# A new order for a fused gated-linear-attention and bilinear-FFN kernel: alphas sent a block early, decays by pairs of heads, all orders searched anew

## The chip, the cores and the metric

One core of a Trainium2 chip. The time is in device microseconds (us) of one execution. TensorE (PE) multiplies matrices and has a separate row in the profile for its weight loads (PEld); VectorE is DVE, ScalarE is ACT, GpSimd is POOL, and SyncE (SP) issues DMAs. Every engine takes its instructions in the order written, and waits at an instruction whose semaphore has not come.

## The reference

Attention with a gated state, then a bilinear feed-forward block (FFN) on all its outputs:

```python
B, H, S, D = 4, 8, 768, 48
state = zeros(B, H, D, D)
for t in range(S):
    state = alpha[:, :, t, :, None] * state + einsum('bhd,bhe->bhde', k[:, :, t], v[:, :, t])
    y[:, :, t] = einsum('bhd,bhde->bhe', q[:, :, t], state)

x = y.transpose(0, 2, 1, 3).reshape(3072, 384)
out = (x @ w_a) * (x @ w_b) @ w_out     # w_a, w_b: 384 x 1536, w_out: 1536 x 384
```

Inputs and output are float32.

## The kernel before

The sequence is cut into 3 stretches of 256 positions, and the 4 batches into 2 pairs: six chunks of 512 rows. Chunk c holds stretch c // 2 and batches 2 * (c % 2) and the next. One position in two is an "even" row (r = 0), the other "odd" (r = 1), and 128 such pairs lie on the partitions; 64 of them make a group g.

For a chunk, the attention part runs in these steps, each a name in a program text:

- `ld` loads alpha, k, q or v. `ln` takes the logarithm of alpha (ACT, L586), `A` or (`l2`, `H`, `L`, `A2`, `le`) add it up along the sequence on PE with a triangle of ones. `E` takes exponentials (ACT, L646): `beta` is the decay from the start of the group, `invb` its inverse.
- `mk` and `mq` multiply keys by `invb` and queries by `beta` (DVE, L650) into `QKp`. They are turned so that the head dimension lies on the partitions: `C` on PE (L690) with the copy `Ce` (L696, L698) for chunks 0 and 1, and `T`, a DMA transpose issued by SP (L701), for chunks 2 to 5.
- `D` makes scores on PE (L758), `M` masks them (DVE, L763), `SB` and `SA` add the carried state (L774), `Y` the inner products (L774), and `X` copies the result to `xT` (L809).
- `K` and `k` make the new state (L729, L743 to L747). The decay of a whole group, `bl`, comes from the last row of `beta`: `dk` and `de` do that on PE and a copy for chunks 0 and 1, `dec` by a DMA through DRAM (L655, L658) for the others.

The FFN part has, for each of 12 column blocks f of 128, `a` and `b` (PE, L825, three matmuls each), `as` (ACT copies a, L831), `pr` (DVE multiplies by b, L838 or L841), then `o` (PE, L848) for 4 row blocks m, `ot` (a copy, L856 or L858) and `st` (the store, L865). With `*` a step of `a` takes all 512 columns, with 0 or 1 half of them (256): the halves let the first FFN work start when half of `xT` is there.

`x v S` and the like end with the engine's letter: V is DVE, S is ACT, P POOL, Y SP. A number at the end is the PSUM bank. Weights come by `W` and `Wo`, cast during the DMA, which POOL issues. `warm` is a matmul on zeros that has no other purpose than to run. `gatet` is a copy of one element on POOL that waits for a turned key, so that loads after it are not sent while the transposes run.

The order of all of this on every engine is the order of a text, `PROGRAM`, that the kernel interprets: `c: op; op; ...` for chunk c. Nothing else schedules it; waits come from the data and the buffers. Here are the steps around the gates of chunk 2 before:

```
2: K * 6; gatet 0
...
2: gatet 1
...
3: ld a * P
...
3: ld k * P
```

All loads of a chunk go to two buffers for each of a, k, q and v. `beta` and `invb` have one buffer each. The PSUM has eight banks that the text names by hand.

Of the kernel before, what the change touches and what calls it, by code (L numbers as in the profile page):

```python
# [18 lines left out]
0: ld a 0 Y; ld a 1 Y; cm 0; cm 1; ld k 0 Y; ld v 0 Y; cS 1 V; cQ 1 V; cM 0 V; cV 0 V; ln 0; ld q 0 P; cM 1 V; A 0 1 4; ld k 1 P; cQ 0 V; ln 1  # L19
0: cS 0 V; ld q 1 P; A 0 0 2; E 0 i1; ld v 1 P; E 0 b1; A 1 1 5  # L20
1: ld a 0 P
0: E 0 i0; E 0 b0; mk 0 V
1: ld a 1 P
0: A 1 0 4; E 1 i1; v 0 V; W b 0 256; E 1 b1; mq 0 V; dk 0 6; W a 0 256; E 1 i0; K 0 0; E 1 b0; dk 1 7; W a 256 1024; C 0 0 2; de 0 S; mk 1 V
0: W b 256 1024; de 1 S; Ce 0 0 S; C 0 1 7
1: ld k 0 P
0: k 0 0 V; warm 2 3; k 0 1 V; Ce 0 1 S; D 0 0 2
1: ld v 0 P
0: warm 2 4; mq 1 V; SB 0 0
1: ld q 0 P  # L30
0: D 0 1 6; v 1 S; M 0 0; C 1 0 5; W a 1024 1536; warm 2 4; Ce 1 0 S; M 0 1; W b 1024 1536; K 1 2; C 1 1 4; Wo 0 6; k 1 0 V; D 1 0 6; Ce 1 1 S
1: ld k 1 P
0: Y 0; SA 0; k 1 1 V; M 1 0
1: ld q 1 P
0: SB 1 4; D 1 1 2; X 0 S; Wo 6 12
1: ln 0
0: M 1 1
1: ld v 1 P; ln 1
0: a 0 0 6
# [3 lines left out]
0: as 0 0  # L43
1: H 0 V; L 0 V
0: b 0 0 6; X 1 S
2: ld k * P
1: l2 1 V; A2 0 1; H 1 S; le 0
2: ld q * P
1: E 0 b1
0: pr 0 0; a 6 * 7  # L50
1: E 0 i1; L 1 V
0: a 7 * 5
2: ld v * P
1: E 0 b0
0: cV 1 V; a 0 1 3; a 1 0 0; as 0 1; b 0 1 4; as 1 0; b 1 0 2; pr 0 1; as 6 *; a 3 0 1; pr 1 0
1: A2 1 6
0: as 3 0; b 6 * 3
1: le 1; E 0 i0
0: b 3 0 0
1: E 1 b1  # L60
0: pr 6 *; b 7 * 1; as 7 *
1: mk 0 V
0: a 4 * 2
1: E 1 i1
0: a 3 1 3; pr 3 0; b 3 1 7; as 3 1
1: dk 0 4
0: pr 7 *; as 4 *; b 4 * 6; pr 3 1
1: v 0 S
0: a 5 * 0
1: mq 0 V  # L70
0: b 5 * 7; as 5 *
1: de 0 V; C 0 1 3
0: pr 4 *; a 2 0 1
1: Ce 0 1 S; C 0 0 2
0: pr 5 *; b 2 0 4; a 8 * 5
1: Ce 0 0 V
0: as 2 0
1: E 1 b0; K 0 6
0: pr 2 0; as 8 *
1: D 0 0 2  # L80
0: a 11 * 0
1: k 0 0 V; M 0 0
0: b 11 * 4; as 11 *; a 10 * 5
1: k 0 1 V; E 1 i0; SB 0 2; D 0 1 0
0: as 10 *; b 8 * 6
1: M 0 1
0: b 10 * 7
1: dk 1 5
0: pr 8 *
1: Y 0; SA 0; de 1 S  # L90
0: pr 11 *; a 9 * 0; pr 10 *
1: X 0 S
0: b 9 * 6; as 9 *
1: b 11 0 3; a 1 0 2
0: pr 9 *
1: a 2 0 0; as 1 0; b 1 0 4; mk 1 V; as 2 0
0: a 2 1 1
1: b 2 0 6
0: as 2 1
1: a 4 0 2; pr 1 0  # L100
0: b 2 1 5
1: pr 2 0; as 4 0; a 8 0 7
0: pr 2 1
1: b 4 0 1; as 8 0; a 6 0 6; pr 4 0; b 6 0 2; as 6 0; mq 1 V; b 10 0 7; b 8 0 0; a 9 0 6; pr 8 0
0: a 1 1 5
1: as 9 0
0: b 1 1 1
1: pr 6 0
0: as 1 1
1: a 11 0 4; b 9 0 0  # L110
0: pr 1 1
1: as 11 0; C 1 0 6; pr 9 0; v 1 S; a 10 0 2; Ce 1 0 V; a 5 0 5; C 1 1 4; as 10 0; pr 11 0; as 5 0; K 1 0; pr 10 0; D 1 0 2
0: o 1 0 5
1: k 1 0 V; M 1 0
2: ln *
0: o 2 0 7; o 2 1 -
1: Ce 1 1 S
2: l2 * V
1: a 0 0 3; k 1 1 V
0: o 1 1 -  # L120
2: H * S
1: as 0 0
2: L * V
1: SB 1 0
0: ot 2 S
1: b 5 0 3
0: ot 1 S
1: pr 5 0
2: A2 0 7
1: D 1 1 4  # L130
2: le 0; E 0 i1
1: b 0 0 2
2: E 0 b1; A2 1 6
1: M 1 1
0: o 0 0 3
2: E 0 b0; E 1 b1; le 1
1: Y 1; SA 1
2: E 1 i1; dec; mq 0 V; E 0 i0
0: o 0 1 -
1: X 1 S  # L140
2: mk 0 V; E 1 i0
1: b 3 0 6; pr 0 0; b 11 1 0
2: E 1 b0; T 0
1: a 3 0 1
2: mk 1 V
1: a 8 1 4; as 3 0; a 11 1 2; as 8 1; a 9 1 5; pr 3 0; as 11 1; a 4 1 1
2: mq 1 V
1: b 8 1 4
0: ot 0 S
1: a 7 0 6; as 9 1; b 9 1 7; pr 11 1  # L150
2: T 1; v 1 S
1: b 7 0 3; pr 8 1; a 7 1 5
0: st 0 YY
2: v 0 V
1: b 2 1 0; as 4 1; b 7 1 2; as 7 0; pr 9 1; b 4 1 4; a 3 1 1; as 7 1
0: st 2 YY
1: pr 4 1
2: K * 6; gatet 0
1: pr 7 0; as 3 1; pr 7 1
2: D 0 0 4  # L160
0: st 1 YY
1: a 2 1 3
2: k * 0 V
0: o 3 0 2
1: as 2 1
2: M 0 0
1: a 0 1 3
0: o 3 1 -
2: gatet 1
1: as 0 1  # L170
3: ld a * P
2: k * 1 V
1: b 0 1 3
0: ot 3 S
1: b 3 1 5
3: ld k * P
1: a 1 1 4; pr 3 1; a 6 1 2; pr 2 1; a 5 1 7; as 1 1
3: ld q * P
1: a 10 1 1; pr 0 1; as 5 1; b 1 1 5; as 10 1; b 10 1 4; pr 1 1; b 5 1 7
3: ld v * P  # L180
1: pr 10 1; b 6 1 6; as 6 1
2: D 1 0 0
1: pr 5 1
2: SB 0 4
1: pr 6 1
2: D 0 1 2
1: o 2 0 7
2: M 0 1
1: o 2 1 -
2: M 1 0  # L190
3: ln *
2: Y 0; SA 0
1: ot 2 S
3: l2 * V
2: SB 1 0; D 1 1 2; X 0 S
1: o 1 0 6; st 2 YY
3: H * V
1: o 0 0 5
0: st 3 YY
3: L * V  # L200
1: o 1 1 -
2: M 1 1
3: A2 0 4
1: ot 1 S
3: A2 1 7; le 0
2: Y 1; SA 1
3: E 0 b1
1: st 1 YY
3: le 1; E 0 b0
1: o 0 1 -  # L210
3: mq 0 V
2: X 1 S
3: E 1 b1
2: b 11 * 0
1: ot 0 V
3: E 1 b0; dec
2: a 11 * 3
3: E 1 i1; mq 1 V
2: a 0 * 1
3: E 1 i0  # L220
2: as 11 *; b 6 * 7
3: mk 1 V; E 0 i0
2: a 6 * 5; pr 11 *; as 0 *
3: T 1
2: b 0 * 2; as 6 *
3: v 1 V
2: a 7 * 3
3: E 0 i1
2: pr 0 *; a 4 * 6
3: v 0 S; mk 0 V  # L230
2: a 5 * 5; as 7 *; b 7 * 2; pr 6 *
3: T 0
2: as 4 *; a 1 * 4; pr 7 *; as 5 *; b 5 * 7; as 1 *; b 4 * 3; pr 5 *; b 1 * 2; pr 4 *
3: D 1 0 6
2: pr 1 *
3: K * 4; M 1 0
2: a 2 * 1; b 2 * 3
3: gatet 0
2: as 2 *
3: gatet 1; k * 0 V  # L240
4: ld a * P
2: a 10 * 0; a 3 * 6; as 10 *
4: ld k * P
3: k * 1 V
1: o 3 0 2
2: as 3 *
4: ld q * P
2: pr 2 *
3: SB 1 0; D 1 1 6; D 0 0 4
1: o 3 1 -  # L250
3: M 1 1
4: ld v * P
2: a 8 * 3
3: M 0 0
1: ot 3 S
3: Y 1; SA 1
2: as 8 *
3: SB 0 2; D 0 1 4; X 1 S
2: b 8 * 7
3: M 0 1  # L260
4: ln *
2: b 9 * 6; a 9 * 0; pr 8 *
3: Y 0; SA 0
4: l2 * V
2: b 10 * 1
4: H * V
3: X 0 S
2: b 3 * 4
4: L * V
3: b 11 * 2  # L270
2: pr 10 *
3: a 8 * 7
2: pr 3 *
3: b 8 * 3; as 8 *
4: A2 0 5
2: as 9 *
4: A2 1 1; le 0
3: b 0 * 7
4: E 1 b1
3: pr 8 *  # L280
2: o 2 0 4
4: E 0 b0
2: pr 9 *
4: E 0 i1
3: a 1 * 3
4: E 0 b1; le 1; E 1 i1
3: a 0 * 0
4: dec; mq 0 V; E 0 i0
3: a 6 * 6
4: E 1 b0; mk 0 V  # L290
2: o 2 1 -
3: as 6 *
4: v 1 V; E 1 i0
3: b 4 * 1
4: T 0
2: ot 2 S
4: mk 1 V
2: o 1 0 6
3: as 1 *
4: mq 1 V  # L300
3: as 0 *
2: o 1 1 -
4: v 0 S; T 1
3: b 6 * 5
1: st 0 YY
3: a 11 * 3; pr 6 *; b 1 * 4
2: ot 1 V
3: as 11 *
2: st 2 YY
3: a 4 * 0; pr 1 *  # L310
4: gatet 0
3: a 5 * 3; pr 0 *; as 4 *
1: st 3 YY
3: b 3 * 6; pr 11 *; as 5 *; a 10 * 4; pr 4 *; b 5 * 0; as 10 *
4: gatet 1
3: a 3 * 5
5: ld a * P
3: pr 5 *; a 2 * 1; as 3 *; b 10 * 3
5: ld k * P
3: as 2 *; pr 3 *  # L320
4: K * 4
3: pr 10 *
4: D 0 0 0
5: ld q * P
4: D 1 0 6
3: a 7 * 2
4: M 1 0
5: ld v * P
2: o 0 0 3
3: as 7 *  # L330
# [12 lines left out]
2: ot 0 S; o 3 1 -
5: l2 * V
4: SB 1 2; D 1 1 6
3: b 7 * 1
5: H * S
4: M 1 1; Y 0; SA 0
2: ot 3 S
5: L * V  # L350
2: st 3 YY
4: Y 1; SA 1; X 0 S
3: pr 7 *
2: st 1 YY
5: A2 1 7
4: X 1 V
5: A2 0 0; E 1 b1
3: o 0 0 6
5: E 0 i1; le 0; E 1 i1
4: b 9 * 4  # L360
5: le 1; E 0 b1
3: b 9 * 2
5: E 0 b0; dec
4: a 8 * 7
5: E 1 i0
3: pr 9 *
5: E 1 b0
4: a 9 * 5
5: E 0 i0; mq 1 V
3: o 1 0 0  # L370
4: as 9 *
2: st 0 YY
5: mq 0 V; v 1 S
3: o 0 1 -
4: pr 9 *
3: o 1 1 -; ot 0 S
5: mk 0 V
4: a 3 * 5
3: ot 1 S
5: mk 1 V  # L380
4: a 6 * 6
5: T 0
4: as 3 *; b 8 * 1
3: st 1 YY
4: as 8 *
5: v 0 V
4: a 0 * 0; as 6 *
5: T 1
4: b 3 * 2; b 6 * 3; pr 3 *
3: o 2 0 4  # L390
4: pr 6 *; as 0 *; pr 8 *; b 0 * 5; a 1 * 6; pr 0 *
5: K * 2; D 0 0 0
4: a 2 * 7
5: M 0 0
3: o 2 1 -
4: as 2 *
5: k * 0 V
4: a 4 * 0
3: ot 2 S
4: b 2 * 7; as 4 *; b 4 * 2; as 1 *; pr 2 *  # L400
5: D 1 0 0
4: pr 4 *
5: SB 0 4; D 0 1 6
4: a 11 * 3
5: M 1 0
3: o 3 0 2
4: as 11 *
5: M 0 1
4: b 11 * 1
3: o 3 1 -  # L410
4: pr 11 *
5: Y 0; SA 0
3: ot 3 V; st 3 YY
5: SB 1 2; D 1 1 6; X 0 S
4: a 10 * 0
5: M 1 1
3: st 0 YY
4: a 7 * 1; b 1 * 5
3: st 2 YY
5: Y 1; SA 1  # L420
4: pr 1 *; b 5 * 7
5: X 1 S
4: a 5 * 5; as 7 *
5: b 11 * 2
4: as 5 *; b 7 * 1; as 10 *; pr 5 *; b 10 * 3
5: a 1 * 6
4: pr 10 *
5: a 11 * 4
4: pr 7 *; o 1 0 3
5: as 11 *; as 1 *  # L430
4: o 3 0 7
5: b 1 * 0; b 5 * 4; pr 1 *; a 5 * 1; pr 11 *
4: o 3 1 -
5: as 5 *; pr 5 *; b 9 * 0
4: ot 3 V; o 0 0 6; st 3 YY
5: b 3 * 7; a 3 * 5; a 9 * 1; as 3 *
4: o 0 1 -
5: pr 3 *; a 2 * 5
# [12 lines left out]
4: o 2 1 -
5: as 10 *; b 8 * 6; pr 10 *
4: ot 2 S
5: o 0 0 4; as 8 *
4: st 2 YY
5: pr 8 *; o 1 0 5; o 0 1 -; o 2 0 7; ot 0 S; st 0 YY; o 1 1 -; o 2 1 -; ot 1 V; st 1 YY; o 3 0 1; ot 2 S; o 3 1 -; st 2 YY; ot 3 SV; st 3 YS
"""


@with_exitstack  # L460
def kernel(
# [11 lines left out]
    nc = tc.nc  # L473
# [493 lines left out]
```

## Time and profile before

| what | value |
|---|---|
| median of 3 runs | 203.47 us (201.44 to 203.55) |
| the profiled execution | 202.53 us |
| its span, first to last instruction | 200.7 us |
| PE busy | 189.5 us, 94% |
| DVE, ACT, POOL busy | 138.3, 103.9, 39.6 us |
| loads by POOL (q0), by SP (q1) | 20.84 MB, 10.44 MB |
| granted clock | 0.994 |

The page lists, for one execution, the busy time of each engine, DMA queues, the chain that ended last, and groups of like instructions. A matmul's end is modelled, so its duration says little; the spacing between starts says what it costs. Stretches count the busy time of each engine in a part of the span. A line of the timeline gives start, duration, engine, line, operation, and in brackets the idle time of the engine before it and what ended it; "issue" there is a wait that no semaphore explains.

### The profile page before, as it was taken

Reading aid. Unit: us, or ns where it says so; the run is one execution under the profiler, and the core shown is the slowest. Engines: PE = TensorE matmul, PEld = TensorE weight load, DVE = VectorE, ACT = ScalarE, POOL = GpSimd, SP = SyncE. Lnnn points to the kernel's source line nnn. Section 1 sums busy time; section 2 is a strip of 40 time slices with the busy share of each in tenths; the row PEclk is TensorE's granted clock in tenths of the full one; section 3 lists DMA queues with packets and bytes.
Section 4 is the critical chain, followed back from the end, with each engine's and each line's share of the span. In section 5 each row is a group of like instructions: output and inputs, shape, how many; then the busy total and the mean of one; then the engine's idle time right before and its main releaser. Section 6 shows DMA issues by size and latency. Waiting matters only on the chain.

```text
span 200.7 us, 5861 instructions
## 1 busy us (share of the span) xinstructions
PE 189.5 (94%) x2516; PEld 113.2 (56%) x2516; DVE 138.3 (69%) x217; ACT 103.9 (52%) x196; POOL 39.6 (20%) x58
## 2 busy tenths in 40 slices
PE   7997589999999999799999999999999999999991
PEld 2565455668767886544565554565555655544560
DVE  6599669768978886887978867897758734352510
ACT  3576767645868544386353855447714242233310
POOL 7974536400000080000620005300000000000000
PEclk9999999999999999999999999999999999999997
DMA  6999999999702959959399298996591140103124
GB/s 163 270 262 216 233 253 203 257 283 265 205 0 20 215 128 318 262 146 193 60 275 264 58 168 156 282 264 170 86 177 33 27 94 0 42 0 78 39 59 98
DMA packets 39593, 31.74 MB, mean 158 GB/s; under 512 B 28424, under 2 KB 35336, under 8 KB 39568
## 3 DMA queue, kind: packets, MB, share of 16 engines
q0 software_dynamic: 8640, 20.84, 43.8%
q1 hardware_dynamic: 30848, 10.44, 25.9%
q8 instruction: 19, 0.31, 0.7%
q10 hardware_dynamic: 80, 0.10, 0.1%
q14 instruction: 6, 0.05, 0.1%
HBM read 25.98 MB, written 4.74 MB: 153 GB/s over the span
## 4 chain that ended last, share of the span: by engine, by line
PE 83%; DMA 6%; ACT 3%; issue 3%; DVE 2%; ACTq 0%; POOLq 0%; POOL 0%
PE psum L825 44%; PE psum L848 20%; PE psum L774 5%; DMA a_t<-in_alpha_dram 3%; PE psum L616 3%; PE psum L610 3%; PE psum L758 2%; DMA kqT<-QKp 2%; PE psum L690 2%; PE psum L729 2%; PE psum L634 2%; PE psum L666 1%; ACT xT L809 1%; ACT invb L646 1%; ACT beta L646 1%
## 5 line engine op out<-in xcount | busy, mean ns | idle before, releaser
L825 PE MATMUL psum<-xT,wa_t 128*128 128x512 bf16 (+1 forms) x264 | 56.6, 341 | 0.7 <-ACT xT L809 0.7
L825 PE MATMUL psum<-xT,wb_t 128*128 128x512 bf16 (+1 forms) x264 | 57.0, 341 | 0.1
L848 PE MATMUL psum<-wo_t,prod 128*128 128x384 bf16 x288 | 52.1, 326 | 0.6 <-ACT xT L809 0.6
L848 PEld LDWEIGHTS <-prod 128*128 128x128 bf16 x288 | 27.4, 98 | 20.9 <-issue 1.2
L825 PEld LDWEIGHTS <-wa_t 128*128 128x128 bf16 x264 | 25.0, 98 | 20.3 <-issue 0.6
L825 PEld LDWEIGHTS <-wb_t 128*128 128x128 bf16 x264 | 25.0, 98 | 19.3 <-issue 0.6
L763 DVE TENSOR_TENSOR m<-psum,mask 128x1024 bf16<-128x1024 f32 x24 | 28.9, 1220 | 5.7 <-PE psum L758 4.9
L856 ACT ACTIVATE ot<-psum 128x384 f32<-128x384 f32 (+1 forms) x18 | 8.6, 478 | 13.6 <-PE psum L848 13.6
L878 POOL CAST go<-kqT 1x1 f32<-1x1 bf16 x6 | 1.0, 173 | 72.0 <-DMA kqT<-QKp 71.9
L809 ACT ACTIVATE xT<-psum 128x768 bf16<-128x768 f32 x11 | 8.9, 809 | 10.8 <-PE psum L774 10.8
L650 DVE TENSOR_TENSOR QKp<-k_t,invb 128x768 bf16<-128x768 f32 x12 | 11.4, 954 | 3.0 <-ACT invb L646 2.6
L586 ACT ACTIVATE la<-a_t 128x768 f32<-128x768 f32 (+1 forms) x8 | 9.2, 1159 | 6.6 <-DMA a_t<-in_alpha_dram 6.6
L774 PE MATMUL psum<-m,vx 64*64 64x128 bf16 x576 | 10.6, 218 | 1.4 <-issue 1.2
L650 DVE TENSOR_TENSOR QKp<-q_t,beta 128x768 bf16<-128x768 f32 x12 | 11.3, 952 | 0.8 <-DMA q_t<-in_q_dram 0.8
L774 PEld LDWEIGHTS <-vx 64*64 64x64 bf16 x576 | 8.7, 107 | 4.6 <-issue 4.5
L758 PE MATMUL psum<-kqT 64*64 64x128 bf16 x384 | 9.8, 218 | 0.2 <-ACT kqT L696 0.2
L646 ACT ACTIVATE invb<-psum 128x384 f32<-128x384 f32 x14 | 6.7, 490 | 4.4 <-PE psum L616 2.3
L578 POOL DMA_DIRECT2D q_t<-in_q_dram x8 | 8.3, 1034 | 3.5 <-DMA wb_t<-in_moe_w_b_dram 2.7
L646 ACT ACTIVATE beta<-psum 128x384 f32<-128x384 f32 x14 | 6.8, 488 | 3.9 <-DVE la L637 3.0
L858 DVE COPY ot<-psum 128x384 f32<-128x384 f32 (+1 forms) x7 | 3.7, 527 | 7.5 <-PE psum L848 4.7
L637 DVE TENSOR_TENSOR la<-psum,la 128x384 f32<-128x384 f32 x10 | 5.4, 555 | 4.4 <-PE psum L634 3.4
L758 PEld LDWEIGHTS <-kqT 64*64 64x64 bf16 x384 | 6.8, 106 | 2.1 <-issue 1.3
(243 smaller groups left out, 260.0 us busy)
## 6 DMA issues: line engine op xcount, KB each, us to landing
out_dram<-ot SPq DMA_DIRECT2D x47, 96.0 KB, 3.0
a_t<-in_alpha_dram POOLq DMA_DIRECT2D x4, 768.0 KB, 6.9
k_t<-in_k_dram POOLq DMA_DIRECT2D x4, 768.0 KB, 9.2
q_t<-in_q_dram POOLq DMA_DIRECT2D x4, 768.0 KB, 11.7
v_t<-in_v_dram POOLq DMA_DIRECT2D x4, 768.0 KB, 13.3
q_t<-in_q_dram POOLq DMA_DIRECT2D x4, 384.0 KB, 10.0
k_t<-in_k_dram POOLq DMA_DIRECT2D x3, 384.0 KB, 14.4
v_t<-in_v_dram POOLq DMA_DIRECT2D x3, 384.0 KB, 14.0
```

Source lines behind the costliest of these rows:

```text
L578: eng.dma_start(out=t[:, us].rearrange("p b h r d -> p (b h) (r d)"), in_=src[ch.b0 + us.start:ch.b0 + us.stop, :, ch.s * 2 * C:(ch.s + 1) ...
L586: nc.scalar.activation(out=ch.la[:, us].rearrange("p b h r d -> p (b h r d)"), in_=ch.a[:, us].rearrange("p b h r d -> p (b h r d)"), func ...
L610: nc.tensor.matmul(w, lhsT=wz[:, :C], rhs=wz, start=True, stop=True)
L646: nc.scalar.activation(out=t[:, r, u], in_=src, func=AF.Exp, scale=sc)
L650: eng.tensor_mul(QKp[ch.c % 2][:, u, j, :, :, :D], src[:, u].rearrange("p h r d -> p r h d"), by[:, :, u])
L758: nc.tensor.matmul(s2[g * HC:(g + 1) * HC, r, p, rk, :], lhsT=ch.kqT[u][rs, 1, rk, 2 * h + p, g * HC:(g + 1) * HC], rhs=queriesT(ch, u, 2 ...
L763: nc.vector.tensor_mul(m.rearrange("p r a k s -> p (r a) (k s)"), ch.s2[u, h].rearrange("p r a k s -> p (r a) (k s)"), maskn(4))
L774: nc.tensor.matmul(y[c * DP:(c + 1) * DP, g, j // 2 * C:(j // 2 + 1) * C], lhsT=lhsT, rhs=rhs, start=(g, c) not in begun, stop=False, skip ...
L809: nc.scalar.activation(out=o_, in_=i_, func=AF.Copy)
L825: nc.tensor.matmul(p, lhsT=(wa_t, wb_t)[w][:, kk, f * 128:(f + 1) * 128], rhs=ch.xT[:, kk, us, :], start=(kk == 0), stop=(kk == KT - 1))
L848: nc.tensor.matmul(op, lhsT=ch.prod[:, f, m * C:(m + 1) * C], rhs=wo_t[:, f, :], start=(f == 0), stop=(f == NFF - 1))
L856: nc.scalar.activation(out=ot[:, fs], in_=ch.pf["o", m][:, fs], func=AF.Copy)
```

## The change

`PROGRAM` has a new order throughout. Apart from the order:

- The alphas of chunks 3, 4 and 5 are sent one chunk earlier: chunk 3's stand between chunk 2's queries and values, ahead of the gates of chunk 2.
- `beta` is now a fixed tile with 64 columns for each head in place of 48, the last 16 zero (`const_decays`, step `cB`). So `dk` takes two heads in one matmul (4 of 128 columns in place of 8 of 48), and `de` is one copy in place of two. The DMA of `dec` reads 16 pieces of 48 numbers in place of one row of 768.
- The zeros for `warm` are the first 512 columns of the state tile `S0[0]`, in place of a tile of their own; `warm` is run 13 times, before 16.
- In the fill, q of chunk 0 and the loads behind it are issued by POOL ahead of the masks (`cm`), and after it the row order is r = 0 before r = 1, queries before keys.
- Some copies go to other engines (`de` of chunk 0 from ACT to DVE; single `H`, `X`, `ot` and `v` steps).

```diff
-0: ld a 0 Y; ld a 1 Y; cm 0; cm 1; ld k 0 Y; ld v 0 Y; cS 1 V; cQ 1 V; cM 0 V; cV 0 V; ln 0; ld q 0 P; cM 1 V; A 0 1 4; ld k 1 P; cQ 0 V; ln 1
-0: cS 0 V; ld q 1 P; A 0 0 2; E 0 i1; ld v 1 P; E 0 b1; A 1 1 5
-0: E 0 i0; E 0 b0; mk 0 V
-0: A 1 0 4; E 1 i1; v 0 V; W b 0 256; E 1 b1; mq 0 V; dk 0 6; W a 0 256; E 1 i0; K 0 0; E 1 b0; dk 1 7; W a 256 1024; C 0 0 2; de 0 S; mk 1 V
-0: W b 256 1024; de 1 S; Ce 0 0 S; C 0 1 7
-0: k 0 0 V; warm 2 3; k 0 1 V; Ce 0 1 S; D 0 0 2
-0: warm 2 4; mq 1 V; SB 0 0
-0: D 0 1 6; v 1 S; M 0 0; C 1 0 5; W a 1024 1536; warm 2 4; Ce 1 0 S; M 0 1; W b 1024 1536; K 1 2; C 1 1 4; Wo 0 6; k 1 0 V; D 1 0 6; Ce 1 1 S
-0: Y 0; SA 0; k 1 1 V; M 1 0
-0: SB 1 4; D 1 1 2; X 0 S; Wo 6 12
+0: ld a 0 Y; ld a 1 Y; ld q 0 P; ld k 0 Y; ld v 0 Y; cS 1 V; ld k 1 P; cB V; ld q 1 P; cS 0 V; ld v 1 P; ln 0; cV 0 V
+0: cQ 1 V; A 0 0 3; cM 0 V; ln 1
+0: cM 1 V; cV 1 V; A 0 1 7; E 0 b0; W a 0 256; E 0 i0; cQ 0 V; W b 0 256; A 1 1 0; E 0 b1; cm 0; cm 1; E 0 i1; mq 0 V; A 1 0 5; E 1 b1; mk 0 V
+0: E 1 i1; dk 0 7; v 0 V; E 1 i0; C 0 0 1; E 1 b0; dk 1 3; de 0 V; W a 256 1024; K 0 6; Ce 0 0 S; mk 1 V; C 0 1 5; W b 256 1024; Ce 0 1 S; D 0 0 0
+0: k 0 0 V; warm 2 2; mq 1 V
+0: SB 0 4; warm 1 2; M 0 0; C 1 0 2
+0: v 1 S; W a 1024 1536; k 0 1 V; D 0 1 0; Ce 1 0 S; W b 1024 1536; M 0 1
+0: D 1 0 6
+0: C 1 1 2; M 1 0; de 1 S; K 1 0
+0: Ce 1 1 S; k 1 0 V
+0: SB 1 6; D 1 1 2; Y 0; SA 0; Wo 0 6; M 1 1
...
 2: ld q * P
...
+3: ld a * P
...
 2: ld v * P
...
-3: ld a * P
...
+3: ld k * P
...
+4: ld a * P
...
-    wz = cst.tile([C, 512], BF16, name="wz")
+    wz = S0[0].rearrange("p b e -> p (b e)")[:, :512]
+    beta = cst.tile([C, 2, 2, H, DP], F32, name="beta")
...
+    def const_decays(eng):
+        ENG[eng].memset(beta[:, :, :, :, D:].rearrange("p r b h d -> p (r b h) d"), 0.0)
...
-            nc.sync.dma_start(out=row[g:g + 1].rearrange("g (b a) r d -> g b (a r d)", b=2),
-                              in_=ch.beta[(g + 1) * HC - 1:(g + 1) * HC, 1].rearrange("g b h d -> g b (h d)"))
+            nc.sync.dma_start(out=row[g:g + 1].rearrange("g a r d -> g (a r) d"),
+                              in_=beta[(g + 1) * HC - 1:(g + 1) * HC, 1, :, :, :D].rearrange("g b h d -> g (b h) d"))
...
-        for hd in range(H):
-            p, r = hd // 2, hd % 2
-            nc.tensor.matmul(d[r * DP:r * DP + D, 2 * p:2 * p + 2], lhsT=ch.beta[:, 1, u, hd, :], rhs=last, start=True, stop=True)
+        for p in range(P2):
+            nc.tensor.matmul(d[:, 2 * p:2 * p + 2], lhsT=beta[:, 1, u, 2 * p:2 * p + 2, :].rearrange("s h d -> s (h d)"), rhs=last, start=True, stop=True)
```

In the changed kernel the line numbers are 9 to 14 lower in the functions; `dk` is L656, `E` L637.

## The prediction

> **What bounds the kernel now.** I read the page's busy line and forty slices first, then each engine's busy time by stretches of 5 us, then the chain in order of time, then the timeline of TensorE (PE) where it stops.
>
> ```profile
> PE 189.5 (94%) x2516; PEld 113.2 (56%) x2516; DVE 138.3 (69%) x217; ACT 103.9 (52%) x196; POOL 39.6 (20%) x58
> ...
> q8 instruction: 19, 0.31, 0.7%
> ```
>
> PE is the bound. In the stretches (columns: length, busy time of PE, PEld, DVE, ACT, POOL, clock, DMA share, GB/s) it is full from 30 to 195 us but for one:
>
> ```profile
> 15.00:20.00 5.00, 3.77 (x123) 2.53 (x123) 4.70 (x7) 3.25 (x4) 2.14 (x3) 1.00 1.22 220
> 20.00:25.00 5.00, 2.87 (x123) 2.43 (x112) 3.17 (x5) 3.88 (x6) 2.87 (x4) 1.00 1.15 228
> 25.00:30.00 5.00, 4.20 (x28) 2.77 (x28) 3.18 (x8) 3.02 (x8) 1.71 (x2) 1.00 1.09 254
> ...
> 80.00:85.00 5.00, 3.80 (x70) 2.54 (x68) 4.34 (x6) 2.16 (x5) 0.00 (x0) 1.00 1.03 263
> ```
>
> So only the fill (up to 25.8 us), a stop near 80 us and the drain (4.4 us from the last matmul at 196.3) can be won; 165 us of dense matmuls stay. What stops PE (chain: start, us, what; timeline: idle time in brackets):
>
> ```profile
> 18.50 1.23 issue
> ...
> 24.28 1.52 issue
> ...
> 71.17 7.01 DMA a_t<-in_alpha_dram
> ...
> 79.60 0.47 ACT ot L856
> 80.07 0.71 ACT xT L809
> ...
> 84.43 0.55 issue
> ```
>
> ```profile
> 25.80 0.34 PE L634 MATMUL psum<-lh,utr 128*128 128x384 f32 x1 [2.03 <-issue]
> ```
>
> ```profile
> ACT la L586 <- DMA a_t<-in_alpha_dram: 3.3, 1, 3.3
> ```
>
> The 80 us stop: ScalarE (ACT) works in order. Its log of chunk 3 (L586) waits 3.3 us for alphas that were sent at 71.17, only after the turned keys of chunk 2 had landed; ot and xT queue behind it, and PE needs the bank that xT frees (idle 0.65 us).
>
> The three "issue" stops have no semaphore behind them. They lie exactly 256 instructions apart or a multiple of that: counting PE's matmul and weight-load records, PE resumes at number 449 (19.72 us), 705 (25.80) and 2497 (84.98). Queue q8 carries 19 packets of 16 KB; those in front of these stops ran 16.98 to 18.24, 23.31 to 24.20 and 82.17 to 83.43, and PE resumed 1.5 to 1.6 us after each. PE is waiting for its own instructions. It passed number 193 at 13.12, so a block of 256 took 6.6 and 6.1 us here, though the second holds only 2.3 us of work (spacing of starts by kind of matmul).
>
> **What the Trainium skill says.** "Runtime: NRT & Kernel Launch", Instruction fetch mechanics: instructions come in blocks of 16 KiB (256 instructions) by the sequencer's own DMA queue, while the current block runs, and this is mostly hidden. The trace agrees on size and queue; hidden it is not where a block is short and loads fill the engines. "DMA: Bandwidth & Descriptors", Queues, rings and completion order: each DMA engine serves its queues in turn, packet by packet. The trace agrees: from 7.7 to 8.0 us, when the software queue (POOL) and the hardware queue (SP) both had loads, they moved 49 and 47 KB. "TensorE: Matmul & The Clock Gate", LDWEIGHTS: the time goes by columns, which I use for the decay matmuls.
>
> **The change, part by part.** The program has 797 steps before and after, with the same number of each FFN and attention operation; so the work of PE changes only by the decays, and the rest is a matter of order.
>
> (1) Decays by pairs of heads: each dk goes from 8 matmuls on 48 columns to 4 on 128. An fp32 matmul is two in the records: 16 at a mean spacing of 22.8 ns are 0.37 us. The new shape isn't in the trace; by columns 128/48 x 22.8 = 61 ns, and the nearest row, a 128-column transpose (L690), is spaced 56 ns: 8 x 56 = 0.45. Four dk: 4 x 0.08 = +0.3 us; at 61 ns +0.5; and if the time went by matmuls rather than columns, 8 x 22.8 = 0.18 each, -0.7. I take +0.3, for the columns. The copy out (L673) falls from two instructions of 0.17 us to one: 0.17 us off ACT or DVE, hidden except at 13 us. The 16 fragments in place of one row in the decay's DMA, and strided beta, fall in waits that have cover: bl is wanted some 5 us after it lands. A new memset of beta costs DVE 0.48 us (as QKp's, same width), ahead of 8.3 us, when DVE was free until 9.6. Nothing.
>
> (2) Fill, loads. POOL sends q0 right after the triangle, at 1.8 us in place of 4.69; the masks (2.9 us of POOL) go behind the loads, done by 11.6 and wanted at 15. Software loads flow 2.9 us after their issue starts (4.69 to 7.6), so from 4.7 us they share the engines with SP's k0 and v0. At 1.5 us for each 384 KB alone (landings 4.40, 5.90, 7.41, 8.91), shared halves give q0 at 8.8 (was 10.42), k0 8.9 (7.41), v0 11.9 (8.91), k1 11.8, q1 13.4, the rest as before.
>
> (3) Fill, order. The cumulative sums fill PE to 11.6 as before, 1.29 us each; the row order is 0, 1 and beta first. DVE: mq 9.6 to 10.6 (q0 is there), mk to 11.5, v waits to 11.9 and ends 12.6, de 12.8, second mk 13.7, Sm 14.1, second mq 15.05. PE: dk 0 to 12.05, first turn 12.5; ACT copies it (1.02) to 13.8, where before it ran 13.54 to 14.56; the first scores start at 14.0 (14.62). DVE: M 0 0 15.05 to 16.3, state 17.0, M 0 1 18.2, M 1 0 19.4, state and pair sum 20.3, M 1 1 21.5 (was 22.1). All scores now stand ahead of inner Y 0 on PE: Y 0 from 19.9, in place of 18.2.
> But the block limit holds: 193 now falls in the first scores, 14.0, so 449 (in Y 0) comes no earlier than 14.0 + 6.6 = 20.6, and 705 no earlier than 26.7. Between: Y 0 and its evacuation to 22.2; Y 1 from 21.6; then FFN without a gap from 22.4, since lh, ll (done 23.5) and the second xT (23.3) are ready as they come. By number 705 PE has done 15 FFN matmuls at 108 ns and 9 at 216, 3.6 us, where before it had done 6, 0.65 us; the A2 sums stand even within 0.1. The need of 4.0 us from 22.4 is 26.5, so the limit of 26.7 binds slightly. Weights hold: wb's middle columns land 26.6, b 7 stands near 27.9. Gain 3.6 - 0.65 - (26.7 - 25.8) = 2.0 us. The fewer warming matmuls (13 for 16) stood in waits: nothing.
>
> (4) Alphas. Those of chunk 3 are now sent from POOL right behind chunk 2's queries, ahead of the gates (gatet, a copy on POOL that waits for the turned keys, and behind which every later load of POOL stands). They land about where v of chunk 2 landed, 56 to 59 us; the 3.3 us wait of ACT goes and with it the stop at 79.8: -0.7 (0.65 idle and the refill). They delay chunk 2's v by 2.9 us, from 55.8 to 59; but its casts ran at 65.5 (ACT) and 66.2 (DVE), so 6 us of cover are left: nothing. If that cover were gone, PE's state sums and scores would wait for v by what it is late. Keys and queries after each gate move up one place; DVE's 0.76 us wait for q goes too. The later logs' waits were not PE's. What is late next is the transpose and its matmuls: between T 0 of chunk 2 and its first scores lie 16 half FFN groups (0.33) and one output half (0.98), 6.3 us, where 14 and the state sums made 5.3: more cover for its 4.4 us.
>
> (5) Dense part. The 0.77 us fetch stop at 2497 goes with the old order (its block now holds 8.0 us of work, not 5.3). But in the new order the block from 2753 holds only 5.8 us, and five others 6.3 to 6.7, against the 6.1 to 6.9 that a block took under load. All stops gone would be -0.8, three new ones of that size +1.6; I take half a stop coming back: -0.4.
>
> Sum against the profiled span: -2.0 - 0.7 - 0.4 + 0.3 = -2.8: span 197.9, the execution 202.53 to 199.7. That execution lies 0.9 below the median of the three runs (201.44 to 203.55), so the median goes from 203.47 to 200.7.
>
> **Rivals.** A, the gain is eaten: a new order with 797 steps has handovers I haven't followed, and short blocks stop again at 0.7 us each. For: six short blocks, some of them under loads. Against: in the kernel before, blocks of 5.6 and 6.3 us of work ran without a stop when few loads were flowing (4289 to 4545 took 5.8 us). Three stops cost 2.1, 1.7 more than the 0.4 that I allow: 202.4, within 1%.
> B, slower: v0 starves. Place: v 0 on DVE, in order ahead of mk, mq and every mask. If the software queue is served first, v0 comes behind q0, k1, q1, v1 and a pair of alphas, 16.4 rather than 11.9, and the whole chain from v 0 moves 4.5 us: 200.7 + 4.5 = 205.2, slower than before by 0.9%; with one more fetch stop behind it, as large as the largest before (1.5), 206.7, which I take as its time. The deciding point: v0 later than 14.7 (11.9 + 2.8) takes back all that the change brings. Against it: the equal shares at 7.7.
> C, more: no stop comes back (-0.4), the decays go by matmuls (-1.0), the two blocks of the fill are fetched 0.3 sooner (a block there took 6.1 to 6.6): 1.7 more, 199.0.
>
> **How the numbers follow.** Forecast 0.53, A 0.27, B 0.12, C 0.08. About 1% is what a measurement of this kernel tells from no change, so faster is under 201.4: forecast and C less a little of their edge, 0.60; same 0.28 (A and that edge); slower 0.12. The range holds C, the forecast with the decays' ends (-1.0 and +0.2 about the value taken), the fill's (0.7 either way, half a transfer of 384 KB) and A up to its worse half: 198.6 to 203.6.
>
> **What would show it.** Right: PE's 705th record near 26.7 with 24 FFN matmuls before it; no wait of la for a_t near 80; k0 near 8.9 and v0 near 11.9; L656 spaced near 56 ns. Wrong: v0 after 14 us; "issue" stops that sum to over 2 us after 30 us; ACT or DVE ending new idle times of PE in the dense part.

## The result, and the profile after

| | before | after |
|---|---|---|
| median, beside each other on one chip | 202.9 us (201.44 to 203.55, 4 runs) | 210.93 us (210.41 to 212.47, 4 runs) |
| ratio, with its 95% interval | 1 | 1.042 [1.033, 1.050] |
| profiled execution, its span | 202.53, 200.7 us | 211.25, 209.4 us |
| granted clock | 0.994 | 0.971 |

The kernel is slower by 4.2%, where 200.7 us was forecast. It is rival B, starved values, and larger than its price. In the runs below, ratios are against the kernel before on the same chip, whose median lay between 202.6 and 203.0 us on the three chips used. Medians and ratios leave out executions that ran longer at a lower granted clock than the rest of their kernel, and the traces of *before_masks_late* and *after_warm* are of such executions.

The page of the kernel after, busy line and slices (each digit a fortieth of the span):

```profile
PE 190.0 (91%) x2460; PEld 117.0 (56%) x2481; DVE 136.0 (65%) x217; ACT 104.3 (50%) x193; POOL 40.8 (19%) x58
...
PEclk9995599999999999999999999999999999999998
```

PE has as much busy time as before, in a span 8.7 us longer: it waits more. The stretches (columns as in the prediction) say where:

```profile
10.00:15.00 5.00, 1.86 (x12) 1.38 (x10) 0.01 (x1) 1.56 (x4) 4.55 (x11) 1.00 1.07 262
15.00:20.00 5.00, 2.41 (x16) 2.41 (x16) 0.96 (x1) 1.02 (x1) 2.98 (x4) 0.62 1.24 210
20.00:25.00 5.00, 2.65 (x59) 2.15 (x59) 2.98 (x6) 1.04 (x2) 1.80 (x2) 0.50 1.16 220
25.00:30.00 5.00, 3.66 (x88) 2.25 (x87) 4.13 (x7) 3.45 (x5) 1.71 (x2) 0.85 1.07 263
```

DVE does 0.01 us of work from 10 to 15 us and 0.96 in the next five (4.70 from 15 to 20 before), while the DMA engines move 210 to 263 GB/s, as before (220 to 254): it is not too little that arrives, but the wrong tensor. The granted clock is 0.5 from 16.2 to 26.5 us. The chain that ended last, in order of time, then the waits:

```profile
2.93 18.68 DMA v_t<-in_v_dram
...
22.25 0.70 PE psum L718 x24
22.95 0.97 PE psum L679 x8
```

```profile
DVE vx L704 <- DMA v_t<-in_v_dram: 6.7, 2, 4.1
DVE QKp L641 <- DMA k_t<-in_k_dram: 6.6, 1, 6.6
...
PE psum L679 <- DVE QKp L641: 5.7, 1, 5.7
...
PE psum L718 <- DVE vx L704: 2.0, 1, 2.0
```

Read as a list: v0, 384 KB, was under way for 18.68 us. DVE stands 6.6 us at the product with k0 and 4.1 us at the cast of v0 (the other 2.6 belong to a later chunk); PE's first turn waits for the one (5.7 us), its first state sum for the other (2.0). Landings, from issue and completion of each load: q0 7.56, k1 10.37, q1 12.02, v1 13.69, two pairs of alphas 15.35 and 17.02, all POOL's; SP's k0 16.48 and v0 21.61. Before, k0 and v0 landed at 7.41 and 8.91.

**How much of the loss this is.** One of the runs below, *masks_first*, is the changed kernel with its old load order, and shares everything behind the fill. The timeline of DVE, first of that kernel, then of the kernel after:

```profile
12.41 0.55 DVE L704 CAST vx<-v_t 128x768 bf16<-128x768 f32 x1
...
15.59 1.22 DVE L752 TENSOR_TENSOR m<-psum,mask 128x1024 bf16<-128x1024 f32 x1
...
17.57 2.41 DVE L752 TENSOR_TENSOR m<-psum,mask 128x1024 bf16<-128x1024 f32 x2
```

```profile
21.64 0.56 DVE L704 CAST vx<-v_t 128x768 bf16<-128x768 f32 x1 [4.10 <-DMA v_t<-in_v_dram]
...
24.65 1.23 DVE L752 TENSOR_TENSOR m<-psum,mask 128x1024 bf16<-128x1024 f32 x1 [0.38 <-PE psum L747]
...
27.36 2.41 DVE L752 TENSOR_TENSOR m<-psum,mask 128x1024 bf16<-128x1024 f32 x2 [0.84 <-PE psum L747]
```

The cast comes 21.64 - 12.41 = 9.2 us later, the first mask 9.1, the second pair of masks 9.8. From there every one of the 23 later masks and of the 88 products (`prod`) lags by 9.8 or 9.9 us, up to the last product at 197.9. So the late v0 costs 9.2, the short stretch from v0 to the second masks some 0.6 to 0.7, and the other 180 us contribute nothing: the spans differ by 209.4 - 199.5 = 9.9. The half clock accounts for the short stretch by its matmuls: eight turns took 1.03 us there and 16 scores 0.64, against 0.62 and 0.42 in *masks_first*.

**Why v0 starves.** From 9 to 12 us, when loads waited in both queues (in these lines q0 is POOL's queue and q1 SP's; then packets, MB, share of the engines' time):

```profile
q0 software_dynamic: 206, 0.71, 92.8%
q1 hardware_dynamic: 207, 0.08, 15.2%
```

They go turn for turn. But POOL's packets, up to 4,224 bytes each, carried 713 KB, and SP's, of 384 bytes, 77 KB. From 12 to 15 us it is 205 packets to 204, 706 KB to 78. SP has half of the turns and a tenth of the bytes. The rows are the same in both queues: every load of q, k, v or alpha reads 384 bytes at a time (48 numbers of a head, even and odd together). POOL's packets hold eleven such rows, SP's one. That is the unseen part of the sentence from the Trainium skill, "DMA: Bandwidth & Descriptors", Queues, rings and completion order, on which the prediction rested: an engine drains a whole packet from one queue's ring before it switches. The packet counts agree; halves in packets are not halves in bytes.

### The profile page after: what moved, and what is told of

It reads as the page before. It is cut to its first block, busy times and chain, and to the rows that moved or that the text cites. A ratio compares the mean times of both kernels' runs of the same rounds, so it can differ in the third digit from the quotient of the medians.

```text
span 209.4 us, 5772 instructions
## 1 busy us (share of the span) xinstructions
PE 190.0 (91%) x2460; PEld 117.0 (56%) x2481; DVE 136.0 (65%) x217; ACT 104.3 (50%) x193; POOL 40.8 (19%) x58
## 3 DMA queue, kind: packets, MB, share of 16 engines
q0 software_dynamic: 8640, 20.84, 41.1%
q1 hardware_dynamic: 31088, 10.44, 25.8%
## 4 chain that ended last, share of the span: by engine, by line
PE 66%; DMA 21%; DVE 4%; SPq 3%; issue 2%; POOL 1%; ACT 1%; POOLq 0%; DVEq 0%
PE psum L814 34%; PE psum L837 18%; DMA v_t<-in_v_dram 15%; PE psum L763 5%; DMA kqT<-QKp 4%; PE psum L747 3%; DMA row<-beta 2%; DVE m L752 2%; PE psum L679 2%; PE psum L718 2%; PE psum L623 1%; DVE QKp L641 1%; SPq L567 1%; SPq L690 1%; PE psum L656 1%
## 5 line engine op out<-in xcount | busy, mean ns | idle before, releaser
L814 PE MATMUL psum<-xT,wb_t 128*128 128x512 bf16 (+1 forms) x256 | 55.4, 339 | 0.8 <-issue 0.6
L814 PE MATMUL psum<-xT,wa_t 128*128 128x512 bf16 (+1 forms) x252 | 54.6, 339 | 1.3 <-issue 0.5
L845 ACT ACTIVATE ot<-psum 128x384 f32<-128x384 f32 (+1 forms) x16 | 7.7, 479 | 16.5 <-PE psum L837 16.5
L798 ACT ACTIVATE xT<-psum 128x768 bf16<-128x768 f32 x12 | 9.7, 810 | 9.6 <-PE psum L763 9.4
L685 ACT ACTIVATE kqT<-psum 128x1024 bf16<-128x1024 bf16 x7 | 7.1, 1023 | 13.9 <-PE psum L679 13.9
L679 PE MATMUL psum<-ident,QKp 128*128 128x128 bf16 x64 | 5.8, 244 | 5.7 <-DVE QKp L641 5.7
L637 ACT ACTIVATE invb<-psum 128x384 f32<-128x384 f32 x14 | 6.8, 489 | 4.9 <-DVE la L626 3.1
L847 DVE COPY ot<-psum 128x384 f32<-128x384 f32 (+1 forms) x9 | 4.7, 530 | 6.9 <-ACT ot L845 3.7
```

Source lines behind the costliest of these rows:

```text
L679: nc.tensor.transpose(t[:, j, r, p], QKp[ch.c % 2][:, u, j, r, hp:hp + 2, :].rearrange("s h d -> s (h d)"), ident)
L685: nc.scalar.activation(out=o_, in_=i_, func=AF.Copy)
L798: nc.scalar.activation(out=o_, in_=i_, func=AF.Copy)
L814: nc.tensor.matmul(p, lhsT=(wa_t, wb_t)[w][:, kk, f * 128:(f + 1) * 128], rhs=ch.xT[:, kk, us, :], start=(kk == 0), stop=(kk == KT - 1))
L845: nc.scalar.activation(out=ot[:, fs], in_=ch.pf["o", m][:, fs], func=AF.Copy)
```

## The experiments

**1. The load order alone, both ways.** *masks_first* puts the masks ahead of POOL's loads again, *before_masks_late* does only the opposite to the kernel before.

```diff
# masks_first, against the kernel after (and "cm 0; cm 1" taken out of its later line)
-0: ld a 0 Y; ld a 1 Y; ld q 0 P; ...
+0: ld a 0 Y; ld a 1 Y; cm 0; cm 1; ld q 0 P; ...
# before_masks_late, against the kernel before
-0: ld a 0 Y; ld a 1 Y; cm 0; cm 1; ld k 0 Y; ld v 0 Y; cS 1 V; cQ 1 V; cM 0 V; cV 0 V; ln 0; ld q 0 P; ...
+0: ld a 0 Y; ld a 1 Y; ld k 0 Y; ld v 0 Y; ld q 0 P; cS 1 V; cQ 1 V; cM 0 V; cV 0 V; ln 0; ...
-0: A 1 0 4; ... W a 0 256; E 1 i0; ...
+0: A 1 0 4; ... W a 0 256; cm 0; cm 1; E 1 i0; ...
```

> The changed kernel with one thing put back: POOL makes the masks ahead of the load of q0, as before the change, so its loads start 2.9 us later. Theory S (k0 and v0, in SP's queue with packets of 384 bytes, take turns packet by packet with POOL's packets of 4224 bytes, and starve): k0 lands near 7.5 and v0 near 9.0 instead of 16.5 and 21.6, PE's stops of 5.9 and 2.2 us in the fill go, and the time falls by some 8 us to 201 to 204. Rival O (the searched order, the decays by pairs or the early alphas carry the loss, and the late loads are hidden by something else): the time stays above 207.

> The kernel before with one part of the change alone: the masks stand behind POOL's loads of q, k and v of chunk 0 and alpha of chunk 1, so q0 is sent at 1.8 us. Order, decays and alphas are as before. Theory S: k0 lands near 16.5 and v0 near 21.6, and the time rises by 7 to 9 us, to 210 to 212. Rival O: within 2 us of the kernel before.

*masks_first*: 201.37 us (20 runs), ratio 0.994 [0.991, 0.996]. k0 landed at 7.55, v0 at 9.06. *before_masks_late*: 212.7 us (2 runs, 211.14 and 214.23), 1.051 [1.039, 1.062], k0 at 16.68 and v0 at 22.52. The timeline of PE in the latter, where its first state sum stands:

```profile
11.21 0.53 PE L666 MATMUL psum<-last,beta 128*48 128x2 f32 x16
23.16 0.64 PE L729 MATMUL psum<-vx,QKp 64*64 64x48 bf16 x32 [11.42 <-DVE vx L715]
```

Two steps moved by a few microseconds on POOL are the whole loss, in either program. The masks' 2.9 us had been holding POOL's queue shut while SP's loads went through. With the old load order the rest of the change makes the kernel 0.6% faster (0.4 to 0.9).

**2. Packets, or a queue served first?** The share could also come from POOL's queue, the software one, being preferred. *one_queue* sends k0 and v0 by POOL, so that nothing competes; *big_rows* leaves them with SP, but reads each as 3,072 bytes in a row for a partition; these two tiles then hold other values than the kernel needs, in the same number of bytes.

```diff
# one_queue, against the kernel after
-... ld q 0 P; ld k 0 Y; ld v 0 Y; ...
+... ld q 0 P; ld k 0 P; ld v 0 P; ...
# big_rows, in load(), against the kernel after
+        if eng is nc.sync and what in ("k", "v"):
+            flat = src[ch.b0 + us.start].rearrange("h s d -> (h s d)")[:C * H * 2 * D]
+            eng.dma_start(out=t[:, us].rearrange("p b h r d -> p (b h r d)"), in_=flat.rearrange("(p x) -> p x", p=C))
+            return
```

> The changed kernel with k0 and v0 issued by POOL too, in the order q0, k0, v0, k1, q1, v1. In one queue nothing takes turns. Theory S: landings 1.5 us apart, q0 7.6, k0 9.1, v0 10.6; the fill is as the prediction had it, PE dense from about 23 us, and the time is 200 to 203 (the prediction's 200.7 plus about 1 to 2 for the decays by pairs, whose matmuls were spaced 112 ns and not 56). Rival O: above 207. Rival W (the DMA engines start software loads too late or too slowly whatever the queue): v0 still after 14 us and the time above 205.

> The changed kernel, but SP's loads of k0 and v0 read 3072 contiguous bytes for each partition in place of 8 runs of 384 (so the values in these two tiles are others than the reference's; the number of bytes and all that is done with them are the same). Theory T (queues take turns packet by packet, so a queue's share of the bytes goes by the size of its packets): with packets of up to 3 KB against POOL's 4.2 KB k0 has some 40% of the rate, lands near 9.4 and v0 near 12 to 13, close to what the prediction took, and the time is 201 to 204. Rival P (software loads come first whatever the sizes): k0 still near 16, v0 near 21, and the time near 210.

*one_queue*: 200.59 us (5 runs), 0.991 [0.988, 0.994]; q0, k0, v0 landed at 7.29, 8.79, 10.30. *big_rows*: 200.78 us (14 runs), 0.991 [0.988, 0.994]; q0, k0, v0 at 8.13, 9.29, 12.30. With long rows SP's queue gets its share from the same engines at the same time. From 8 to 9 us the trace of *big_rows* has these packets, the first line POOL's queue:

```profile
q0 software_dynamic: 47, 0.20, 67.5%
q1 hardware_dynamic: 47, 0.14, 41.4%
```

That is 198 KB to 138. So the size of the packets decides, and no preference for a queue. The prediction's 8.8, 8.9 and 11.9 are nearly what the long rows give. DVE's wait for v0 is 0.87 us there, where it was 4.10:

```profile
12.32 0.56 DVE L708 CAST vx<-v_t 128x768 bf16<-128x768 f32 x1 [0.87 <-DMA v_t<-in_v_dram]
```

**3. The low clock.** Did the half clock carry the rest? *after_warm* fills PE's first wait with warming matmuls.

```diff
-0: E 1 i1; dk 0 7; v 0 V; E 1 i0; C 0 0 1; ...
+0: E 1 i1; dk 0 7; v 0 V; E 1 i0; warm 24 1; C 0 0 1; ...
```

> The changed kernel with 24 more warming matmuls in front of the first turn, where PE waits 5.9 us for keys; its clock fell to 0.5 there, from 16 to 26 us. If the low clock carries part of the loss (about 1.4 us of PE's own work on the chain in that stretch ran at half speed): 1 to 2 us faster than the changed kernel, 209 to 210, with the clock at 1.0 until 20 us or later. If the loads alone set the pace: within 0.5 us of it.

216.35 us (3 runs), 1.070 [1.063, 1.078]: 5.4 us slower than after, which neither theory had. The traced execution took 219.06 us, at a mean clock of 0.961. Its stretches:

```profile
10.00:15.00 5.00, 5.00 (x28) 2.83 (x27) 0.00 (x0) 1.52 (x4) 4.55 (x11) 1.00 1.07 261
15.00:20.00 5.00, 3.48 (x26) 2.18 (x25) 0.96 (x1) 1.02 (x1) 2.94 (x4) 0.96 1.24 209
20.00:25.00 5.00, 1.33 (x39) 1.27 (x39) 1.94 (x5) 0.00 (x0) 1.91 (x2) 0.50 1.15 220
25.00:30.00 5.00, 4.46 (x61) 2.38 (x62) 3.17 (x5) 2.97 (x4) 2.31 (x3) 0.50 1.08 261
30.00:35.00 5.00, 4.36 (x137) 3.70 (x137) 3.94 (x6) 2.86 (x6) 2.54 (x3) 0.50 1.17 256
```

The warming held the clock at 1.0 to 19.6 us; PE then waited 4.4 us for v0, and the clock stayed at 0.5 to 36.6 with PE at work from 25 on. In the kernel after, about half of the low clock, to 21.6 us, fell before v0 was there, when it cost nothing. The Trainium skill ("TensorE: Matmul & The Clock Gate", Part 1) gives about 3.4 us of sustained work for the clock to return; here 10 us with PE busy for 4.4 of each 5 did not bring it back. Why not stays open.

The low clock is not what made the kernel slower in its other executions: these had mean clocks of 0.979 to 0.984, above the 0.963 to 0.972 of the kernel after, and were still 4.8 to 7.3 us longer. No trace of them was kept. In the one that was, DVE lags behind the kernel after by 1.4 us at the first mask (v0 landed at 23.04, for 21.61), by 4.6 at the first FFN products, and by 2.0 and then 1.2 more from where PE stops for 3.3 and 1.4 us without a releaser: the matmuls also moved the blocks of instructions. So this run does not settle the price of the half clock; the 0.6 to 0.7 us above is what shows of it.

**4. The decays by pairs.** *one_queue_dk8* is *one_queue* with the old 8 matmuls of 48 columns and two copies.

```diff
-        for p in range(P2):
-            nc.tensor.matmul(d[:, 2 * p:2 * p + 2], lhsT=beta[:, 1, u, 2 * p:2 * p + 2, :].rearrange("s h d -> s (h d)"), rhs=last, start=True, stop=True)
+        for hd in range(H):
+            p, r = hd // 2, hd % 2
+            nc.tensor.matmul(d[r * DP:r * DP + D, 2 * p:2 * p + 2], lhsT=beta[:, 1, u, hd, :D], rhs=last, start=True, stop=True)
```

> As one_queue, with the decays as before the change: eight matmuls of 48 columns and two copies, in place of four of 128 and one. If the pairs cost what the spacing in the changed kernel says (8 records at 112 to 129 ns, 0.9 to 1.0 us, against 16 at 22.8, 0.37), each of the two in the dense part gives back 0.5 us, and the two in the fill as much or nothing: 1.0 to 2.2 us faster than one_queue. If the records' spacing hides an overlap: within 0.4 us of it.

203.78 us (18 runs), 1.005 [1.002, 1.008], 3.2 us slower than *one_queue*, although a dk itself is shorter (the 3.8 of a later expectation is by the median of all 20, 204.39). Spacing in the kernel after: 112 ns between most records of the new form, in the timeline

```profile
10.91 0.95 PE L656 MATMUL psum<-last,beta 128*128 128x2 f32 x8
```

which is 8 x 112 = 0.9 us for a dk, against 16 x 22.8 = 0.37 of the old form. In the traces the old form gives back 0.2 and 0.4 us at the two dk of the dense part, by DVE's products. The waits of PE in *one_queue_dk8* show what outweighs the gain:

```profile
PE psum L765 <- issue: 2.3, 1, 2.3
PE psum L623 <- issue: 1.4, 1, 1.4
```

Both lie where a block of instructions begins (PE's records 704 and 2492), at 25.40 and 84.88 us, each 1.5 us after the end of its 16 KB packet. In *one_queue* the longest "issue" of PE is 0.2 us. The old form has 32 matmul records more, and as many weight loads, half of them ahead of the first stop. The traced execution (202.72 us) is of the faster half: about half took 202.6 to 203.2 us, the others 204.3 to 204.9. What parts the two is not known, so the traces show 1.8 of the 3.2 us.

**5. The place of the blocks alone.** If so, any records of no weight should move the stops. *dk8_shift*, *one_queue_shift* and *before_shift* put 96 matmuls of two columns in place of 5 of the first 10 warming matmuls: 182 records more, ahead of all work, in time that waits anyway.

```diff
-0: c1; warm 10 0
+0: c1; tiny 96 0; warm 5 0
+    def tiny(n, i):
+        for _ in range(n):
+            nc.tensor.matmul(bank(i)[:, :2], lhsT=wz[:, :C], rhs=wz[:, :2], start=True, stop=True)
```

> one_queue_dk8 (eight decay matmuls in place of four) with the same 96 small matmuls. Theory F: what made it 3.8 us slower than one_queue by the median were two fetch stops (1.7 us at record 704, 2.5 us at 2492) that its 16 more records for each decay step brought, not the decays themselves, whose PE time is shorter; with the boundaries moved the stops go from these places and it falls by 2 to 5 us, to 199 to 202. Rival D (the pairs of heads are worth 3.8 us in some other way, as the single copy out): it stays at 203 or more.

> one_queue with the same 96 small matmuls. Theory F: in one_queue the fill ran against the block limit (PE slow from 20 to 23 us and number 705 at 26), so up to 1 us falls away there; later boundaries move by 182 records and can cost or save a stop of up to 2.5 us: 198 to 202. Rival: no change from one_queue beyond 0.5 us.

> The kernel before with 5 of the 10 first warming matmuls replaced by 96 of two columns, in the time when PE waits for alpha anyway. They do nothing but move every later instruction of PE by 182 records against the 256-record blocks in which PE's instructions are fetched. Theory F (the issue stops are waits for the next block of instructions): the first two blocks are now crossed while PE still waits, the stops of 1.23 and 1.52 us before the first FFN matmuls go or shrink, and the time falls by 1.5 to 2.7 us, if no new stop appears later. Rival (the stops have another cause in the work itself): within 0.7 us of the kernel before.

| base | its time | shifted | ratio of the shifted to before |
|---|---|---|---|
| *one_queue_dk8* | 203.78 | 201.01 (7 runs) | 0.992 [0.989, 0.995] |
| *one_queue* | 200.59 | 206.52 (4 runs) | 1.020 [1.015, 1.025] |
| the kernel before | 202.55 | 203.56 (11 runs) | 1.006 [1.003, 1.009] |

*dk8_shift* has no "issue" among PE's waits, and is 2.8 us faster: moving the blocks takes away most of the 3.2 us that the old form had lost. By DVE's products 0.8 us of it come in the fill and 2.3 at the second stop, of which 0.9 is lost again later.

*one_queue_shift* lost 5.9 us, more than was expected. By DVE's products in the two traces 2.6 us of it come in the fill, where PE has a stop of 0.8 and the clock is 0.5 from 20.3 to 27.2 us; 1.3 between 70 and 101 us; and 1.6 around a second stop, of 1.1 us. In *one_queue* the clock was 0.5 only from 20.2 to 23.6, and that, not the block limit, is why PE was slow there: the expectation misread it. The two stops explain a third of the loss; which part of the rest is the clock's these runs do not separate.

*before_shift* lost its stop at 25.8 us, and got one of 1.88 in the inner products:

```profile
21.50 0.24 PE L778 MATMUL psum<-m,vx 64*64 64x128 bf16 x2 [1.88 <-issue]
```

so of the gain expected 0.4 us is left after the fill. It then loses 1.2 us between 69 and 77 us, where PE waits 0.95 us for a turned key, as it did not before. The fewer warming matmuls are a side effect of the shift: in *dk8_shift* the full clock begins at 9.3 us, not 5.3, and there is no stretch of 0.5 after it, where *one_queue_dk8* has one from 18.9 to 22.3 us. Moving the blocks changed these three kernels by -2.8, +5.9 and +1.0 us; only in the first do the stops account for most of it.

**6. The alphas alone.** *before_alphas_early* is the kernel before with only the three early loads.

```diff
+3: ld a * P     # between q and v of chunk 2, ahead of its gates
-3: ld a * P     # behind them; the same for chunks 4 and 5
```

> The kernel before with the early alphas alone: those of chunks 3, 4 and 5 stand ahead of the last load (v) of the chunk before. By the prediction's part 4 ScalarE's wait of 3.3 us near 78 us goes, and PE's stop near 80 us (0.65 us) with it: 0.7 us faster. Rival C (with alpha there early, the decays go to DRAM while k, q and v are still being loaded, and their small packets and the transposes behind them on SP come late): no gain, or up to 2 us slower, with PE waiting for turned keys near 95 us.

202.96 us (20 runs), ratio 1.000 [0.997, 1.002]: nothing. Between 79 and 85.5 us PE's timeline of the kernel before has two idle times. The early alphas remove the first,

```profile
80.82 2.11 PE L848 MATMUL psum<-wo_t,prod 128*128 128x384 bf16 x12 [0.65 <-ACT xT L809]
```

and in *before_alphas_early* all that is left is a longer second one:

```profile
84.47 0.21 PE L774 MATMUL psum<-kqT,S 64*64 64x128 bf16 x1 [1.39 <-issue]
```

It was 0.55 before. Counted between the starts of two blocks, record 705 to 2497, PE took 84.98 - 25.80 = 59.2 us before and 84.47 - 25.27 = 59.2 with early alphas. PE came to the end of its block sooner and waited there for the next.

**7. Cover for a turned key.** In the new order PE waits 1.0 us (*one_queue*) to 1.4 us (after) for a turn of chunk 3. One reason is in the DMAs: in the kernel after, the decay of that chunk, sent by SP ahead of the turn, waited 4.8 us from issue (90.66) to its first packet (95.43), with POOL's loads under way. Chunk 2's waited 1.2 us with no loads, but chunk 4's only 1.8 among about as many, so loads alone are not the whole reason. Before, as one row, the decay took 0.7. *one_queue_cover* and *dk8_shift_cover* move two steps of FFN work ahead of the scores that wait.

```diff
+2: a 8 * 6
+1: o 3 1 -
 ...
-2: a 8 * 6
-1: o 3 1 -
```

> one_queue with one FFN block (a 8, three matmuls) and one output half (o 3 1, six) moved ahead of chunk 3's first scores, where PE waited 1.0 us for turned keys that came late behind decays sent during the loads. Theory C (that stop is the price of the decays' new place among the loads, and 1.6 us of work hides it): 0.6 to 1.2 us faster than one_queue, 199.4 to 200. If the masks behind the scores, now 1.6 us later, hold up the next steps instead: no gain.

> dk8_shift (keys and values of chunk 0 in POOL's queue, eight decay matmuls, instruction blocks moved by 182 records) with the same two pieces of work ahead of chunk 3's first scores: all parts that gained, together. Its stop there was 0.8 us: 0.5 to 1.0 us faster than dk8_shift, near 200.2. If block boundaries, which the move doesn't change in number, fall badly: no gain or slower.

200.41 us (4 runs), 0.989 [0.985, 0.993], and 200.92 us (8 runs), 0.991 [0.988, 0.994]: 0.2 and 0.1 less than their bases, not to be told from nothing: the gain of theory C did not come. The stop is gone, and PE waits for DVE's masks in its place (*one_queue_cover*, waits):

```profile
PE psum L814 <- DVE m L752: 0.5, 2, 0.3
PE psum L763 <- DVE m L752: 0.5, 1, 0.5
```

*one_queue_cover* has the lowest median of all, 1.1% under the kernel before; *one_queue*, two letters away from the kernel after, is as good within its interval.

## Why the prediction was wrong, by its steps

The kernel before, from 7.7 to 8.0 us, where the prediction read how two queues share (SP's queue, then POOL's):

```profile
q1 hardware_dynamic: 134, 0.05, 82.4%
q0 software_dynamic: 12, 0.05, 63.2%
```

- **Step 2, loads: the step that failed.** "Shared halves" was read in bytes from these 0.3 us, in which POOL's queue had barely started: 12 packets to 134, so not even turns show there. With both queues full it is halves in packets, and 77 KB to 713 over 3 us. k0 landed at 16.5 for 8.9 and v0 at 21.6 for 11.9. (The sum also starts the halves at 5.9 us, when the second alpha had landed, and not at the 4.7 that it names; from 4.7 they give k0 10.1 and v0 13.1, still ahead of its deciding point.) The working had the means to see it: the page of the kernel before lists 30,848 packets for 10.44 MB of SP's queue and 8,640 for 20.84 MB of POOL's, 338 bytes against 2.4 KB on average.
- **Rival B** named the place (v0 on DVE, ahead of every mask) and the deciding point (14.7 us). Its v0 at 16.4 lets SP's two loads through as soon as POOL's are done; in fact k0 landed at 16.48, and v0 shared the engines with POOL's alphas (to 17.02) and weights for 5.1 us more. With v0 5.2 us later, and without the fetch stop of 1.5 that B added and that did not come, B's own sum gives 206.7 + 5.2 - 1.5 = 210.4, for 210.9. Its mechanism, the software queue served first, is not what happens: the queues take turns. Its chance of 0.12 stood on the same 0.3 us.
- **Step 3, the order of the fill: right,** once the loads come as it had them. In *one_queue_cover*, the same as *one_queue* up to there, PE passes record 705 at 26.6 us with 24 FFN matmuls before it, as forecast (26.7, 24); in the trace of *one_queue*, with its 0.5 clock from 20.2 to 23.6, near 27.5. Neither stops for the block there. Counted in columns of FFN work, in traces that miss no FFN record, 10,240 are done at 30.11 us before, at 27.51 in *one_queue_cover* and at 28.29 in *big_rows*: 2.6 and 1.8 us, for the 2.0 of the sum.
- **Step 1, decays: mis-sized.** 112 ns for 56: a dk costs 0.5 us more by its spacing, not 0.08 (in the dense part DVE saw 0.2 and 0.4). The row taken as nearest was a bf16 transpose; these are float32. The Trainium skill's price in "TensorE: Matmul & The Clock Gate", LDWEIGHTS, of P / 1.2 ns gives an estimate of 107 for 128 columns, close to the 112, and would have been the better bound. It gives 40 for 48 columns, where the trace has 22.8. The decay's DMA, put at nothing, waited 4.8 us for its first packet in chunk 3, and its turned key came late by 1.0 to 1.4 us (run 7).
- **Step 4, alphas: the mechanism right, the gain not.** The 3.3 us wait of the log and PE's stop went, but the 0.7 us was counted without the block limit that the prediction itself had used for the fill. In the kernel before it turned into the next stop (run 6); in the new order it was not tried alone.
- **Step 5, the dense part:** the stops are waits for blocks of instructions, as supposed (runs 4 and 5). The net of steps 1, 4 and 5 was to be -0.8 us. From 10,240 columns to the last FFN matmul PE took 195.96 - 30.11 = 165.9 us before, 166.3 in *one_queue_cover*, 165.9 in *big_rows*: 0 to +0.4. So even with the loads mended the change is worth less than forecast: 0.9% in *one_queue* (0.6 to 1.2), for 1.4%. That its 200.59 meets the 200.7 is in part luck: the kernel before ran at 203.04 beside it, and the forecast started from 203.47.

The prediction's own signs answer so: v0 after 14 us, wrong; L656 at 56 ns, wrong; no wait of the log near 80, right; "issue" stops over 2 us, not so in the kernel after; PE's new idle time in the dense part was ended by a DMA, the turned key of chunk 3, and not by ACT or DVE.

## What to carry to other kernels

Before an early load is sent beside an urgent one on another queue, compare the bytes of one packet of each in the trace: with turns by packet, packets of 384 bytes got a tenth of the bytes that packets of 4,224 got. The rows in the program don't tell it; here they were the same. Put urgent loads into one queue in the order of need, give them long rows, or hold the other queue back until they are through: each of the three brought this kernel back under 202 us. And where PE runs dense, count its instructions in blocks of 256: a microsecond that is saved ahead of a late block can be given back there, as in run 6, and some 30 to 180 records more can bring a stop of 1 to 2 us or take it away.

## What the runs showed of the hardware

- With loads waiting in both, two DMA queues alternated by packets very evenly (206 to 207, 205 to 204 in 3 us), so their shares in bytes differed 9 to 1. The same rows of 384 bytes went eleven to a packet in POOL's queue and one to a packet in SP's.
- A small DMA sent by SP while POOL's loads ran had its first packet 4.8 us after its issue in one chunk and 1.8 in another, 1.2 without loads.
- A float32 matmul record of 2 columns on 128 weight columns was spaced 112 ns, on 48 columns 22.8: not in proportion to the columns.
- The granted clock was 0.5 in and after waits of PE of several microseconds (after: 16.2 to 26.5 us), but also from 20.2 to 23.6 us in *one_queue*, where no wait of PE in the ten microseconds before was over 0.8 us. In one execution it stayed there for over 10 us of work (run 3).
